# RWKV attention and a top-1 expert layer in one kernel: decay tables doubled from their middle, weight sums behind later transposes, other banks at two seams

## The chip, the cores and the metric

The kernel runs on one core of a Trainium2 chip. The metric is the device time of one execution in microseconds (us). Engines are named as in the profile: PE is TensorE (PEld its weight loads), DVE is VectorE, ACT is ScalarE, POOL is GpSimd, and SP only issues DMAs.

## The reference

```python
# B, H, S, D = 4, 8, 768, 48; for every (b, h), over t:
cur = (u * k[t])[:, None] * v[t][None, :]
y[t] = r[t] @ (state + cur)
state = w[:, None] * state + k[t][:, None] * v[t][None, :]
# x = y as (B*S, H*D) = (3072, 384); 8 experts, F = 1024
logits = x @ w_gate
e = argmax(logits); gate = softmax(logits)[e]
out = gate * (relu(x @ w1[e]) @ w2[e])
```

The decay `w` lies between 0.85 and 0.95 for every channel. All data are float32.

## The kernel before

**First half, the recurrence.** The 768 steps of a head are cut into G = 6 chunks of C = 128. Two heads make a unit, and there are U = 16 units (four head pairs for each of four batches). For a unit, `scale` (L261) multiplies r and k (tile `rk`) by a table `TT` of powers of the decay, so that the products inside a chunk become matmuls (`p_scores`, L292, into the PSUM banks X01[0], X01[1] and X23, which has two banks, X23[:, 0] and X23[:, 1]). `pairs` (L267) and `p_own` (L280) make the step's own term, `own_t` (L284) transposes it, `keys` (L271), `p_ds` (L315) and `scan` (L320) carry the state from chunk to chunk, `p_out` (L335, L340) adds both parts, and `p_tr` (L353) transposes the result into `tr` and X23, from which `keep` (L358, L359, on ScalarE) copies it into `xb`.

The table has two halves of 128 columns for each head pair: for r the powers of w from -64 to 63, for k the same powers backwards. `pw[:, l]` holds w to the power 2^l, from seven squarings on VectorE (L129), `inv` the reciprocal of the 64th power (L133). `decays` (L145, L148) starts each half with `inv` and doubles the filled part seven times, each time with one product by `pw[:, l]`. `state_decay` (L174, L175) fills `dec` from `pw[:, 7]` on GpSimd, and `key_decay` (L152) makes a further table from the same power.

Input loads are issued by SP in the order `w`, then `rk` and `vk` of units 0, 1, 2; a later `load_rk` waits until its buffer is free. `p_fill` (L109) issues matmuls of the identity that nothing reads: 25 of them while the first inputs load, 8 more before unit 1.

**Routing.** After each batch `choose`, `gates`, `p_rank` and `slots` find the expert and the row of every token, and `send` (L407) scatters the rows of `xb` to `rows` in HBM by indirect DMA from GpSimd, one for each chunk.

**Second half, the experts.** A `Pass` computes one expert over some rows. Two `early` passes (experts 0 and 1, 160 rows each, all from the first three batches) are mixed into the end of the first half; eight `late` passes follow. `L1` (L474, L476) computes relu(x w1): block f of eight goes to bank `hbank[f % 4]`, where hbank = X01[0], X23[:, 0], X01[1], X23[:, 1], and ScalarE applies the ReLU. `L2` (L558, L560) is the second layer for early passes and for remainders: three output blocks m, each in its bank (`ybank` = yps[0], dsb, yps[1] for early passes), each followed by a VectorE transpose. In early[0].L2 the argument `first` holds the eight `weight_sums` of late[0] (VectorE sums of blocks of w2 into `tums`, L684), which stand behind the transpose of block 0.

The late passes compute both layers with fewer products from sums of blocks (a form of Strassen's method): `quarter` (L496) for the first layer, with the banks `quads`, and `tokens_out` (L598) for the second, with five banks `self.banks` = ba, bb, bd, be, bf; `so` and `yt` (L616, L623, L627) are the combinations that VectorE and ScalarE make from them, and `scatter` (L670) writes the rows of the output. In late[1] bf is `zbank[2]`, that is X23[:, 0].

**What sets the order.** Every engine executes its instructions in the order in which the program lists them (a schedule written out by hand); semaphores make them wait for each other. The tiles of the second half (`tums` among them) lie in the memory of the first half's tiles (`xb` among them), so their first writer waits for the last reader.

Of the kernel before, what the change touches and what calls it, by code (L numbers as in the profile page):

```python
# [1 line left out]

# [10 lines left out]
ALU = mybir.AluOpType  # L13
# [9 lines left out]
C = 128  # L23
# [5 lines left out]
KP = 64 + D  # L29
# [10 lines left out]
def bc(ap, shape):  # L40
    return ap.to_broadcast(shape)


def straight(tc, rk, vk, w, w1, w2, out, flag):
# [8 lines left out]
    nc = tc.nc  # L53
# [8 lines left out]
    X01 = [pp.tile([128, 4, C], FP32, name=f"X{i}") for i in range(2)]  # L62
    X23 = pp.tile([128, 2, 512], FP32, name="X23")
    yps = [pp.tile([128, 512], FP32, name=f"yps{k}") for k in range(2)]
    dsb = pp.tile([128, 512], FP32, name="dsb")
    tr = pp.tile([128, 512], FP32, name="tr")
# [3 lines left out]
    hbank = [X01[0].rearrange("p a b -> p (a b)"), X23[:, 0, :], X01[1].rearrange("p a b -> p (a b)"), X23[:, 1, :]]  # L70
    ybank = [yps[0], dsb, yps[1]]
    zbank = hbank[0::2] + [X23[:, 0, :]]
# [33 lines left out]
    def p_fill(n, o):  # L106

        for _ in range(n):
            nc.tensor.matmul(o, lhsT=ident, rhs=ident, start=True, stop=True, skip_group_check=True)  # L109
# [7 lines left out]
        nc.sync.dma_start(rows.rearrange("(e n) c -> e (n c)", e=E)[:, PAD * HP * Q:CAP * HP * Q].rearrange(  # L117
            "e (p z) -> p e z", p=128), bc(zt[:, None, :], [128, E, nz]))

    p_fill(25, X01[1][:, 0, :])  # L120
    strict = cp.tile([128, C], FP32, name="strict")
    nc.gpsimd.memset(strict, 1.0)
    nc.gpsimd.affine_select(out=strict, in_=strict, pattern=[[1, C]], base=-1, channel_multiplier=-1,
# [1 line left out]

    pw = cp.tile([KP, 8, HP], FP32, name="pw")
    nc.vector.tensor_scalar(out=pw[:, 0, :], in0=wt, scalar1=W_LO, scalar2=W_HI, op0=ALU.max, op1=ALU.min)
    for l in range(7):
        nc.vector.tensor_tensor(pw[:, l + 1, :], pw[:, l, :], pw[:, l, :], op=ALU.mult)  # L129
    TT = cp.tile([KP, HP, 2, C], FP32, name="TT")  # L130
    TTf = TT.rearrange("p a u c -> p (a u c)")
    inv = cp.tile([KP, HP], FP32, name="inv")
    nc.vector.reciprocal(inv, pw[:, 6, :])  # L133

    T3c = cp.tile([KP, HP, C], FP32, name="T3c")
    T3 = cp.tile([128, HP, 2 * D], FP32, name="T3")
# [1 line left out]
    def two(h0, nh, first, second, n):  # L138

        a = TTf[:, h0 * 2 * C + first:h0 * 2 * C + first + n]  # L140
        return bass.AP(a.tensor, a.offset, [list(a.ap[0]), [2 * C, nh], [second - first, 2], [1, n]])

    def decays(h0, nh):

        nc.vector.tensor_copy(two(h0, nh, 0, 2 * C - 1, 1), bc(inv[:, h0:h0 + nh, None, None], [KP, nh, 2, 1]))  # L145
        for l in range(7):
            n = 1 << l
            nc.vector.tensor_tensor(two(h0, nh, n, 2 * C - 2 * n, n), two(h0, nh, 0, 2 * C - n, n),  # L148
                                    bc(pw[:, l, h0:h0 + nh, None, None], [KP, nh, 2, n]), op=ALU.mult)

    def key_decay(h0, nh):
        nc.vector.tensor_tensor(T3c[:, h0:h0 + nh, :], TT[:, h0:h0 + nh, 1, :],  # L152
                                bc(pw[:, 7, h0:h0 + nh, None], [KP, nh, C]), op=ALU.mult)
# [53 lines left out]
    def in_range():  # L207

        nc.vector.tensor_scalar(out=le, in0=wt, scalar1=W_HI, scalar2=None, op0=ALU.is_le)
        nc.vector.scalar_tensor_tensor(out=okw, in0=wt, scalar=W_LO, in1=le, op0=ALU.is_ge, op1=ALU.mult)  # L210
# [132 lines left out]
    def out_t(i):  # L343
        for k in range(2):
            nc.scalar.copy(yTs[i % 3][0:KP, k], yps[k][0:KP, 0:S // 2])
# [5 lines left out]
    def p_tr(i):  # L351
        for c in range(G):
            nc.tensor.matmul(trv[c // 4][:, c % 4, :], lhsT=yTs[i % 3][0:KP, c & 1, (c // 2) * C:(c // 2 + 1) * C],  # L353
                             rhs=sel[:, c & 1, i % HP, :], start=True, stop=True, skip_group_check=True)
# [22 lines left out]
    def p_rank(b):  # L377

        oh = ohs[b % 2]
        nc.tensor.matmul(rp, lhsT=ones, rhs=bc(osum[:, None, :], full), start=True, stop=False, skip_group_check=True)  # L380
        nc.tensor.matmul(rp, lhsT=tri, rhs=oh, start=False, stop=False, skip_group_check=True)
        for k in range(1, G):
            nc.tensor.matmul(rp[:, k:, :], lhsT=ones, rhs=oh[:, 0:G - k, :], start=False, stop=k == G - 1,
                             skip_group_check=True)
# [28 lines left out]
    def ids(b):  # L413
        nc.gpsimd.iota(xbs[b % 2][:, :, :, 2 * D + 1].bitcast(I32), pattern=[[4 * C, G], [1, HP]], base=4 * S * b,
                       channel_multiplier=4)
# [20 lines left out]
    class Pass:  # L436
# [109 lines left out]
            op(y[2], b22, b12, ALU.subtract)  # L546
            op(y[3], b21, y[1], ALU.subtract)

        def L2(self, first=()):

            n, g = self.n - self.c, self.g - self.gc
            if n <= 0:
                return
            y = self.y
            for m in range(DT):
                p = (zbank if self.nt else ybank)[m]
                for f in range(FT):
                    nc.tensor.matmul(p[:, 0:n], lhsT=w2s[self.k % 2][f // 2][:, f % 2, m * 128:(m + 1) * 128],  # L558
                                     rhs=self.h[:, f, self.c:self.n], start=f == 0, stop=f == FT - 1, skip_group_check=True)
                nc.vector.transpose(y[:, 0:g, 32 * m:32 * m + 32], p[:, 0:32 * g].rearrange("p (g j) -> p g j", j=32))  # L560
                for x in first:
                    op(*x, ALU.subtract)

            yo, ix, x = self.yo, self.ix, self.x[:, self.gc:self.g]
            ids = x[:, :, 2 * D + 1].bitcast(I32)
            if not self.nt:
                nc.vector.tensor_copy(ix[:, 0:g], ids)
            else:
                nc.vector.tensor_scalar(out=vm[:, 0:g], in0=pos[:, 0:g], scalar1=float(self.s0 + self.c),
                                        scalar2=bp[:, self.k:self.k + 1], op0=ALU.add, op1=ALU.is_lt)  # L570
                nc.vector.memset(ix[:, 0:g], 1 << 20)
                nc.vector.copy_predicated(ix[:, 0:g], vm[:, 0:g], ids)
            nc.vector.tensor_tensor(yo[:, 0:g, :], y[:, 0:g, :], bc(x[:, :, 2 * D:2 * D + 1], [128, g, 2 * D]), op=ALU.mult)
            if self.nt:
                self.blocks_out()
# [107 lines left out]
    def op(o, a, b, how, eng=None):  # L683
        (eng or nc.vector).tensor_tensor(o, a, b, op=how)  # L684

    early = [Pass(e, 0, EARLY, 0, early_bufs[e]) for e in range(2)]
    late = [Pass(k, EARLY if k < 2 else 0, n, 2) for k, n in enumerate(WIDTH)]
# [7 lines left out]

    selection()
    decays(0, HP)
    scale(0)
    pairs(0, nc.vector)
# [27 lines left out]
    for i in range(1, U):  # L727
        b, k = divmod(i - 6, 4)
# [62 lines left out]
        if i == 14:  # L791
            weights1(0, (2, 3))

    early[0].L1(range(0, 2), [(weights1, 1, 0), (weights1, 1, 1)])
    p_tr(U - 2)
    keep(U - 2)
    nc.gpsimd.tensor_copy(turn, xbs[1][0:1, G - 1, 2, 0:1])
    send(B - 2, range(3, G))
    p_out(U - 1)
    out_t(U - 1)  # L800
    early[0].L1(range(2, 3), [(weights1, 1, 2)])
    p_tr(U - 1)
    keep(U - 1)
    choose(B - 1)
    gates(B - 1)
    ids(B - 1)
    early[0].L1(range(3, 6), [(weights1, 1, 3), (weights2, 0, 0), (weights2, 0, 1)])
    p_rank(B - 1)
    slots(B - 1)
    send(B - 1, range(G))  # L810
# [18 lines left out]

    for p in late[:2]:  # L830
        nc.gpsimd.memset(p.h[:, :, p.n:p.c], 0.0)
    late[1].banks = dsb, yps[1], yps[0], tr, zbank[2]
    sums = [mp.tile([128, FT // 2, 128], FP32, name=f"sums{k}") for k in range(4)]
    so = [mp.tile([128, DM // 2], FP32, name=f"so{k}") for k in range(8)]
    quart = [mp.tile([128, 5, 128], FP32, name=f"quart{q}") for q in range(4)]
# [29 lines left out]
        with nc.allow_low_precision("whole numbers"):  # L865
            nc.vector.tensor_reduce(flag, viol[0:1, 0:2 * E + HP + 2], axis=AX, op=ALU.add)

    early[0].L2(late[0].weight_sums())
    in_range()
    late[0].xT()  # L870
    early[1].L2()
    for x in late[1].weight_sums():
        op(*x, ALU.subtract)
    n = len(late)
# [522 lines left out]
def rwkv5_then_switch(tc, rk, vk, w, w1, w2, out):  # L1397
    nc = tc.nc
    with tc.tile_pool(name="fl", bufs=1) as fl:
        flag = fl.tile([1, 1], I32, name="flag")  # L1400
        with tc.manual_schedule():
            straight(tc, rk, vk, w, w1, w2, out, flag)
            bad = nc.values_load(flag[0:1, 0:1], engines=[ENG.PE, ENG.SP, ENG.DVE, ENG.Activation, ENG.Pool],
                                 min_val=0, max_val=2 * E + HP + 2, skip_runtime_bounds_check_because="a sum of ones and zeros")
        with tc.If(bad > 0):
            general(tc, rk, vk, w, w1, w2, out)
# [48 lines left out]
```

## Time and profile before

| | |
|---|---|
| median of 3 runs | 371.25 us (371.16 to 371.26) |
| the profiled execution | 370.54 us |
| its span | 368.7 us |
| mean TensorE clock granted | 0.993 |
| PE busy, share of the span | 355.2 us, 96% |
| DVE busy | 263.3 us, 71% |
| POOL busy | 201.3 us, 55% |
| ACT busy | 142.9 us, 39% |
| DMA | 65.08 MB, mean 177 GB/s |

The span is the time from the first to the last instruction of the profiled execution; its own time is 1.8 us longer. The list of waits says for each engine which instruction stood idle and what released it (total, times, longest). The chain of waits follows the work that ended last back in time. In a line of the timeline the columns are start, length, engine, line, operation, output <- inputs, shape and count, and in brackets the idle time before it. Matmuls appear as two passes for each fp32 product, and their ends overlap.

### The profile page before, as it was taken

To read this page: it belongs to the slowest core of one execution; us is meant where nothing else is said; L and a number is where in the kernel's file an instruction comes from. 1 tells how busy PE (TensorE), PEld (TensorE's weight loads), DVE (VectorE), ACT (ScalarE), POOL (GpSimd) and SP (SyncE) were. 2 spreads that over 40 slices of the span, in tenths; PEclk is the share of its full clock that TensorE was granted. 3 is DMA by queue.
4 is the path that set the end of the run, shared out by engine and by line. 5 is a ranking of instruction groups with operands and counts; after the bars stand their busy time and mean duration, and the time that the engine had idled before them with its cause. 6 is when DMAs were issued, how large, how long until landed. Compare 5 with 4: busy or idle time off the path is not lost.

```text
span 368.7 us, 9101 instructions
## 1 busy us (share of the span) xinstructions
PE 355.2 (96%) x3371; PEld 336.3 (91%) x3371; DVE 263.3 (71%) x661; ACT 142.9 (39%) x411; POOL 201.3 (55%) x234
## 2 busy tenths in 40 slices
PE   8999999999999998999998999999999999999991
PEld 8788888888888998999998999999999999999891
DVE  8987798798872347593797996797688589685531
ACT  2687878777784300322322312221230321113210
POOL 3387889989874420462115506904931951999341
PEclk9999999999999999999999999999999999999997
DMA  7999797886665876678458316723842843312401
GB/s 194 256 257 244 242 277 258 246 259 216 217 169 186 299 298 133 175 231 241 124 175 198 125 43 208 192 90 117 213 150 96 199 146 127 111 49 87 145 18 52
DMA packets 35206, 65.08 MB, mean 177 GB/s; under 512 B 18618, under 2 KB 19658, under 8 KB 35153
## 3 DMA queue, kind: packets, MB, share of 16 engines
q1 hardware_dynamic: 29648, 49.86, 48.8%
q0 software_dynamic: 3776, 9.84, 7.4%
q10 hardware_dynamic: 1728, 4.72, 3.7%
q8 instruction: 28, 0.46, 0.5%
q14 instruction: 26, 0.20, 0.2%
HBM read 53.29 MB, written 11.40 MB: 175 GB/s over the span
## 4 chain that ended last, share of the span: by engine, by line
PE 84%; DMA 5%; DVE 5%; POOL 2%; issue 1%; ACT 0%; SPq 0%; POOLq 0%; DVEq 0%
PE X L496 12%; PE X L558 10%; PE tr L598 7%; PE yps L598 7%; PE X L292 6%; PE X L474 6%; PE yps L335 6%; PE yps L496 5%; PE tr L353 5%; PE yps L340 3%; PE tr L496 3%; PE dsb L496 3%; DMA rk<-in_rk_dram 3%; PE dsb L598 2%; PE dsb L315 2%; PE dsb L280 2%
## 5 line engine op out<-in xcount | busy, mean ns | idle before, releaser
L670 POOL DMA_INDIRECT out_dram<-yo,ix x28 | 28.4, 1014 | 68.0 <-DVE ia L587 63.8
L298 ACT ACTIVATE A<-ident,own 128x128 f32<-128x128 f32 x192 | 57.9, 390 | 7.2 <-DVE own L284 6.8
L407 POOL DMA_INDIRECT rows<-xb,slot x24 | 30.3, 1261 | 11.9 <-issue 6.8
L558 PE MATMUL X<-hT,w2s 128*128 128x160 f32 (+5 forms) x288 | 36.5, 287 | 0.0
L558 PEld LDWEIGHTS X<-hT,w2s 128*128 128x128 f32 x288 | 36.2, 191 | 0.2
L598 PE MATMUL yps<-tums,sums 128*128 128x192 f32 x184 | 32.4, 326 | 0.0
L598 PEld LDWEIGHTS yps<-tums,sums 128*128 128x128 f32 x184 | 30.3, 190 | 0.0
L292 PEld LDWEIGHTS X<-RK 48*128 48x128 f32 x384 | 23.3, 187 | 6.0 <-issue 5.1
L670 POOL DMA_INDIRECT out_dram<-yt,it x16 | 16.8, 1048 | 22.0 <-DVE so L616 10.9
L292 PE MATMUL X<-RK 48*128 48x128 f32 x384 | 27.6, 284 | 0.6 <-issue 0.6
L261 DVE TENSOR_TENSOR RK<-rk,TT 112x1536 f32<-112x1536 f32 x16 | 27.7, 1730 | 0.2
L267 POOL TENSOR_TENSOR rp<-rk 112x768 f32<-112x768 f32 x15 | 27.2, 1816 | 0.0
L304 DVE COPY_PREDICATED A<-strict,X 128x512 f32<-128x512 int32 x32 | 23.2, 740 | 4.8 <-ACT A L298 4.7
L496 PE MATMUL X<-xT,w1s 128*128 128x208 f32 (+5 forms) x120 | 26.0, 331 | 0.0
L684 POOL TENSOR_TENSOR tums<-w2s,tums 128x384 f32<-128x384 f32 x24 | 24.7, 1030 | 0.4
L335 PE MATMUL yps<-A,vk 128*48 128x128 f32 x384 | 24.0, 274 | 0.0
L496 PEld LDWEIGHTS X<-xT,w1s 128*128 128x128 f32 x120 | 20.9, 190 | 0.0
L335 PEld LDWEIGHTS yps<-A,vk 128*48 128x48 f32 x384 | 20.2, 123 | 0.5
L684 DVE TENSOR_TENSOR sums<-hT 128x512 f32<-128x512 f32 x16 | 17.1, 1066 | 3.6 <-ACT hT L476 3.2
L632 ACT COPY so<-tr 128x192 f32<-128x192 f32 x7 | 2.2, 320 | 44.5 <-PE tr L598 44.5
L598 PE MATMUL tr<-w2s,hT 128*128 128x192 f32 x112 | 19.4, 326 | 0.0
L525 ACT ACTIVATE hT<-hT 128x416 f32<-128x416 f32 (+5 forms) x23 | 12.3, 537 | 17.7 <-DVE hT L517 17.7
(214 smaller groups left out, 830.3 us busy)
## 6 DMA issues: line engine op xcount, KB each, us to landing
w1s<-in_w_dram SPq DMA_DIRECT2D x36, 384.0 KB, 3.2
rk<-in_rk_dram SPq DMA_DIRECT2D x16, 672.0 KB, 7.5
w2s<-in_w_dram SPq DMA_DIRECT2D x24, 384.0 KB, 3.6
vk<-in_vk_dram SPq DMA_DIRECT2D x16, 528.0 KB, 8.3
w2s<-in_w_dram ACTq DMA_DIRECT2D x8, 384.0 KB, 5.2
xs<-rows SPq DMA_DIRECT2D x16, 169.0 KB, 5.4
w1s<-in_w_dram ACTq DMA_DIRECT2D x4, 384.0 KB, 3.0
rows<-zt SPq DMA_DIRECT2D x1, 1248.0 KB
```

The costliest lines, as they stand in the source:

```text
L261: nc.vector.tensor_tensor(RKs[i % 3][0:KP].rearrange("p u (c t) -> p u c t", t=C), x[0:KP].rearrange("p u (c t) -> p u c t", t=C), bc(TT[: ...
L267: (eng or nc.gpsimd).tensor_tensor(rps[i % 2][0:KP], x[0:KP, 0], x[0:KP, 1], op=ALU.mult)
L292: nc.tensor.matmul(o, lhsT=r[q, 1, c * C:(c + 1) * C], rhs=r[q, 0, c * C:(c + 1) * C], start=True, stop=True, skip_group_check=True)
L298: nc.scalar.activation(A[:, place(c, h), :], ident, func=ACT.Copy, scale=own[i % 2][:, c, h:h + 1])
L304: nc.vector.copy_predicated(A[:, 4 * k:4 * k + 4, :], bc(m[:, None, :], [128, 4, C]), X01[k])
L335: nc.tensor.matmul(o(c, h), lhsT=v[:, c, h * D:(h + 1) * D], rhs=A[:, place(c, h), :], start=c < 2, stop=c == 0, skip_group_check=True)
L407: s_ = nc.gpsimd.indirect_dma_start(out=rows[:, :], out_offset=bass.IndirectOffsetOnAxis(ap=slot[b % 2][:, c:c + 1], axis=0), in_=xbs[b % ...
L496: nc.tensor.matmul(p[:, at * n:(at + 1) * n], lhsT=a, rhs=b, start=j == 0, stop=j == len(ab) - 1, skip_group_check=True)
L558: nc.tensor.matmul(p[:, 0:n], lhsT=w2s[self.k % 2][f // 2][:, f % 2, m * 128:(m + 1) * 128], rhs=self.h[:, f, self.c:self.n], start=f == 0 ...
L598: nc.tensor.matmul(p[:, at * Z:(at + 1) * Z], lhsT=a(f), rhs=b(f), start=f == 0, stop=f == FT // 2 - 1, skip_group_check=True)
L670: s_ = nc.gpsimd.indirect_dma_start(out=to[:, :], out_offset=bass.IndirectOffsetOnAxis(ap=at, axis=0), in_=x, in_offset=None, bounds_check ...
L684: (eng or nc.vector).tensor_tensor(o, a, b, op=how)
```

## The change

Four places are changed.

1. The table is doubled from the power 0 in its middle: GpSimd sets the middle column to 1 and makes the seven squares, VectorE makes six doublings (powers 0 to 63) beside them, and one product by `inv` makes the powers -64 to -1. The first group of fills has 17 matmuls instead of 25.
2. `early[0].L1` gets its banks from a list: blocks 0 to 2 use X01[0], X01[1], X01[0], and blocks 3 to 5 use X01[1], X01[0], X23[:, 0].
3. The eight weight sums of late[0] stand behind later transposes: three behind block 1 of early[0].L2, two behind block 0 and three behind block 1 of early[1].L2.
4. In late[1].tokens_out the fifth bank bf is `dsb` (which is ba as well) instead of X23[:, 0].

```diff
--- before.py
+++ after.py
@@ -1,4 +1,5 @@
 from contextlib import ExitStack
+from itertools import islice
 
 import concourse.bass as bass
 import concourse.tile as tile
@@ -117,7 +118,7 @@
         nc.sync.dma_start(rows.rearrange("(e n) c -> e (n c)", e=E)[:, PAD * HP * Q:CAP * HP * Q].rearrange(
             "e (p z) -> p e z", p=128), bc(zt[:, None, :], [128, E, nz]))
 
-    p_fill(25, X01[1][:, 0, :])
+    p_fill(17, X01[1][:, 0, :])
     strict = cp.tile([128, C], FP32, name="strict")
     nc.gpsimd.memset(strict, 1.0)
     nc.gpsimd.affine_select(out=strict, in_=strict, pattern=[[1, C]], base=-1, channel_multiplier=-1,
@@ -125,12 +126,9 @@
 
     pw = cp.tile([KP, 8, HP], FP32, name="pw")
     nc.vector.tensor_scalar(out=pw[:, 0, :], in0=wt, scalar1=W_LO, scalar2=W_HI, op0=ALU.max, op1=ALU.min)
-    for l in range(7):
-        nc.vector.tensor_tensor(pw[:, l + 1, :], pw[:, l, :], pw[:, l, :], op=ALU.mult)
     TT = cp.tile([KP, HP, 2, C], FP32, name="TT")
     TTf = TT.rearrange("p a u c -> p (a u c)")
     inv = cp.tile([KP, HP], FP32, name="inv")
-    nc.vector.reciprocal(inv, pw[:, 6, :])
 
     T3c = cp.tile([KP, HP, C], FP32, name="T3c")
     T3 = cp.tile([128, HP, 2 * D], FP32, name="T3")
@@ -142,11 +140,18 @@
 
     def decays(h0, nh):
 
-        nc.vector.tensor_copy(two(h0, nh, 0, 2 * C - 1, 1), bc(inv[:, h0:h0 + nh, None, None], [KP, nh, 2, 1]))
+
+        m = C // 2
+        nc.gpsimd.memset(two(h0, nh, m, C + m - 1, 1), 1.0)
         for l in range(7):
+            nc.gpsimd.tensor_tensor(pw[:, l + 1, :], pw[:, l, :], pw[:, l, :], op=ALU.mult)
+        for l in range(6):
             n = 1 << l
-            nc.vector.tensor_tensor(two(h0, nh, n, 2 * C - 2 * n, n), two(h0, nh, 0, 2 * C - n, n),
+            nc.vector.tensor_tensor(two(h0, nh, m + n, C + m - 2 * n, n), two(h0, nh, m, C + m - n, n),
                                     bc(pw[:, l, h0:h0 + nh, None, None], [KP, nh, 2, n]), op=ALU.mult)
+        nc.vector.reciprocal(inv, pw[:, 6, :])
+        nc.vector.tensor_tensor(two(h0, nh, 0, C + m, m), two(h0, nh, m, C, m),
+                                bc(inv[:, h0:h0 + nh, None, None], [KP, nh, 2, m]), op=ALU.mult)
 
     def key_decay(h0, nh):
         nc.vector.tensor_tensor(T3c[:, h0:h0 + nh, :], TT[:, h0:h0 + nh, 1, :],
@@ -546,7 +551,7 @@
             op(y[2], b22, b12, ALU.subtract)
             op(y[3], b21, y[1], ALU.subtract)
 
-        def L2(self, first=()):
+        def L2(self, between=(), count=(0, 0, 0)):
 
             n, g = self.n - self.c, self.g - self.gc
             if n <= 0:
@@ -558,7 +563,7 @@
                     nc.tensor.matmul(p[:, 0:n], lhsT=w2s[self.k % 2][f // 2][:, f % 2, m * 128:(m + 1) * 128],
                                      rhs=self.h[:, f, self.c:self.n], start=f == 0, stop=f == FT - 1, skip_group_check=True)
                 nc.vector.transpose(y[:, 0:g, 32 * m:32 * m + 32], p[:, 0:32 * g].rearrange("p (g j) -> p g j", j=32))
-                for x in first:
+                for x in islice(between, count[m]):
                     op(*x, ALU.subtract)
 
             yo, ix, x = self.yo, self.ix, self.x[:, self.gc:self.g]
@@ -791,20 +796,22 @@
         if i == 14:
             weights1(0, (2, 3))
 
-    early[0].L1(range(0, 2), [(weights1, 1, 0), (weights1, 1, 1)])
+
+    ends = [hbank[k] for k in (0, 2, 0, 2)]
+    early[0].L1(range(0, 2), bank=ends, then=[(weights1, 1, 0), (weights1, 1, 1)])
     p_tr(U - 2)
     keep(U - 2)
     nc.gpsimd.tensor_copy(turn, xbs[1][0:1, G - 1, 2, 0:1])
     send(B - 2, range(3, G))
     p_out(U - 1)
     out_t(U - 1)
-    early[0].L1(range(2, 3), [(weights1, 1, 2)])
+    early[0].L1(range(2, 3), bank=ends, then=[(weights1, 1, 2)])
     p_tr(U - 1)
     keep(U - 1)
     choose(B - 1)
     gates(B - 1)
     ids(B - 1)
-    early[0].L1(range(3, 6), [(weights1, 1, 3), (weights2, 0, 0), (weights2, 0, 1)])
+    early[0].L1(range(3, 6), bank=[hbank[k] for k in (0, 1, 0, 2)], then=[(weights1, 1, 3), (weights2, 0, 0), (weights2, 0, 1)])
     p_rank(B - 1)
     slots(B - 1)
     send(B - 1, range(G))
@@ -829,7 +836,7 @@
 
     for p in late[:2]:
         nc.gpsimd.memset(p.h[:, :, p.n:p.c], 0.0)
-    late[1].banks = dsb, yps[1], yps[0], tr, zbank[2]
+    late[1].banks = dsb, yps[1], yps[0], tr, dsb
     sums = [mp.tile([128, FT // 2, 128], FP32, name=f"sums{k}") for k in range(4)]
     so = [mp.tile([128, DM // 2], FP32, name=f"so{k}") for k in range(8)]
     quart = [mp.tile([128, 5, 128], FP32, name=f"quart{q}") for q in range(4)]
@@ -865,10 +872,11 @@
         with nc.allow_low_precision("whole numbers"):
             nc.vector.tensor_reduce(flag, viol[0:1, 0:2 * E + HP + 2], axis=AX, op=ALU.add)
 
-    early[0].L2(late[0].weight_sums())
+    between = late[0].weight_sums()
+    early[0].L2(between, (0, 3, 0))
     in_range()
     late[0].xT()
-    early[1].L2()
+    early[1].L2(between, (2, 3, 0))
     for x in late[1].weight_sums():
         op(*x, ALU.subtract)
     n = len(late)
```

## The prediction

> **What bounds the kernel now.** I read the page first, for the engine that is nearly always busy, then the list of waits, for where that engine stands still, then the chain of waits and the timeline around each stop.
>
> ```profile
> PE   355.2 (96%) x3371; PEld 336.3 (91%) x3371; DVE 263.3 (71%) x661; ACT 142.9 (39%) x411; POOL 201.3 (55%) x234
> PE 84%; DMA 5%; DVE 5%; POOL 2%; issue 1%; ACT 0%; SPq 0%; POOLq 0%; DVEq 0%
> ```
>
> TensorE is busy for 96% of the 368.7 us span and is 84% of the chain. A change helps only where it removes a stop of TensorE that nothing else holds open. The list of waits has three stops after the first 21 us:
>
> ```profile
> PE dsb L558 <- DVE yqe L560: 1.2, 1, 1.2
> PE X L496 <- DVE yt L623: 1.2, 1, 1.2
> PE X L474 <- ACT xb L359: 0.4, 1, 0.4
> ```
>
> By the timeline they are at 119.8 (L474), 141.0 (L558) and 198.8 us (L496), and the change has an edit at each. The prologue is its fourth place. The chain there:
>
> ```profile
> 2.19 9.89 DMA rk<-in_rk_dram
> 12.08 0.02 issue
> 12.10 1.77 DVE RK L261
> 13.87 0.05 issue
> 13.93 0.18 POOL turn L716
> 14.10 1.78 POOL rp L267
> ```
>
> The first scaling (L261) runs at 7.39, but the chain doesn't pass through it: it goes through the landing of the second `rk` at 12.08, and the second scaling starts 0.02 us later.
>
> [...] the first table product (112x8) took 0.67 us, the next 0.18, and the first ended 0.03 us after the GpSimd copy of `dec` (4.30 to 5.13). [...] at 119.8 us the product into columns 0 to 159 of a half of X23 waited for the ScalarE copy of columns 256 to 359 of that half. [...] The 1.25 us stop at 139.7 left PEclk at 1.00; no longer stop is in the trace.
>
> **Part 1, decay tables and fills.** Removed from VectorE: seven squarings (pitch 0.196 us, 2.81 to 4.15) and the copy (0.17) ahead of the table; seven products become six and a last one by the reciprocal. Added on GpSimd: a memset and seven squarings. The nearest row is the GpSimd 128x8 product of L403, 0.198 us at a pitch of 0.277. From pw[0] at 2.78 the sixth power is then there at 2.85 + 6 x 0.277 = 4.5. The five products before the last two go beside it; the one with n = 32 (0.42) ends by about 4.7, reciprocal (0.17) and last product (512 columns, 0.69) by about 5.6, instead of 7.36. [...] What waits for the table is the first scaling, and it waits for the first `rk` as well:
>
> ```profile
> L93 SPq EVENT_SEMAPHORE x2: 17/908/1798, 7.2 to 12.1; - x2
> ```
>
> SP's own wait for that transfer, queued ahead of the fourth `rk`, ended at 7.2, and the next one at 12.1 plus the scaling. So scaling 0 can gain 0.2 us at most (7.39 to 7.2), and scaling 1 nothing, since `rk` 1 lands at 12.08 with the DMA engines at 96 to 118% busy from 3 to 13 us. Cost taken: 0. Ends: -0.1, and +0.7[...]; the slack before `rk` 1 is only 0.12 us, since VectorE is free for scaling 1 at 11.96. Eight fills fewer (0.22 us each at full clock) end at 7.4 instead of 9.2, and TensorE idles some 1.6 us: nothing, as TensorE has 0.63 us to spare before 15.9 and the clock should hold.
>
> **Part 2, banks of the first expert's first layer.** `ends` and the list after it take blocks 1 and 3 off X23, which `p_tr` writes and `keep` reads in between. Block 3 goes to X01[1], whose last reader is the ReLU of block 1, done at 113.8. TensorE goes on at about 119.21 (the last `p_tr` pass began at 119.10, pitch 0.11) instead of 119.80: **-0.6** (from -0.5 to -0.7, with the slow first pass after a stop). Next candidates: block 4's bank, free with the ReLU of block 2 at 118.4; block 5's, free at 119.7 and needed at 120.8; the rank product needs `oh` at 121.47 and comes at 121.7; block 6's needs the ReLU of block 3, still behind `ex` on ScalarE at 121.3, and comes at 121.9. None is late. ScalarE's weight issues (w2s of expert 0 among them) and GpSimd's six sends start up to 0.6 us earlier; their order is kept.
>
> **Part 3, weight sums behind later transposes.**
>
> ```profile
> 130.38 5.98 DMA rows<-xb,slot
> ...
> 136.57 0.57 DVE tums L684
> ...
> 139.16 1.50 DVE tums L684 x3
> 140.66 0.27 DVE yqe L560
> ...
> 140.97 2.44 PE dsb L558 x16
> ```
>
> `tums` lies where the `xb` being sent lay, so the eight sums wait for the last send to land (136.35) and then hold VectorE until 140.6. Queued behind them is the transpose that empties `dsb`, whose product ended near 135.4, and TensorE stands before its next use of `dsb`. The last pass before the stop began at 139.43; at the pitch of 0.136 the next was due at 139.56 and came at 140.97: 1.41, plus 0.1 for the slow first pass. Now that transpose runs at about 135, ahead of the wait, and three sums follow. The transpose of the third bank runs at 136.3 + 3 x 0.52 = 137.9 and is needed at 141. Next on VectorE are copy, weighting, `in_range` (1.3) and `xT` of the late pass, which waits for `xs`, issued when the sends have landed (0.4 us earlier at best); before, `xs` was in by about 140.6. `xT` (1.0) ends by 141.7, and TensorE needs it at 145.43 - 2.1 = 143.3. The other five sums and their transposes (3.5) stand behind it; the sums of `late[1]` and its `xT` end near 150.3 against 152.4 needed. Gain **-1.45** (from -1.3 to -1.55). No DMA is moved past another.
>
> **Part 4, the last bank of late[1].** `bf` was X23[:, 0], read late by VectorE, so the quarter's third product stood until 198.83. Now it is `dsb`, which is `ba` too:
>
> ```profile
> 194.79 1.46 PE L598 MATMUL X<-tums,hT 128*128 128x192 f32 x8
> ...
> 195.62 0.35 DVE L616 TENSOR_TENSOR so<-dsb,so 128x192 f32<-128x192 f32 x1
> ...
> 198.83 0.62 PE L496 MATMUL X<-toks,quart 128*128 128x206 f32 x2 [1.18 <-DVE yt L623]
> ```
>
> The add that empties `ba` stands at the end of VectorE's backlog and ends at 195.98. The product into `bf`, at 194.79 before, now waits until 196.03. After it come 0.1 of restart, its 8 passes (1.30) and 8 passes of the quarter (1.39): 198.82, where the old order had 198.83 with the restart (0.1) still to pay. The stop moves ahead of the product and is paid anyway: **-0.1** (from -0.2 to +0.3). VectorE's `midu` starts 0.3 later, but the step after it waited 1.6 us for TensorE.
>
> **Sum.** 0 - 0.6 - 1.45 - 0.1 = -2.15 us. Between 200 and 361 us the list of waits has no TensorE stop that could swallow it: weights load as TensorE frees their buffers. The profiled execution had 370.54 (span 368.7 and 1.8 around it), so 368.4. The median of the three runs is 0.71 above it: **369.1**.
>
> **Rivals.**
> - The table was the limit: the whole 1.8 us (7.36 to 5.6) comes through, 367.3. The early end of the fills suits that; the landing at 12.08 is against. Chance 0.05.
> - Only one stop yields: the sends end at 136.35 whatever (the DMA engines are full from 127 to 135), `xs` is later than estimated, or block 3 finds another wait. With Part 3 alone 369.7, with Part 2 alone 370.6. The margins of 1.6 us and more are against it. That an edit does nothing is this case too. 0.14.
> - [...] +0.7, 369.8. The 0.67 us product is for it, the 1.6 us between 5.6 and 7.2 against. 0.09.
> - **Slower: the TensorE clock drops** in the gap from 7.4 to 9.0 and stays low while the first units wait for inputs. Half clock for T us loses T/2 less the 0.63 to spare; it cancels the gain from T = 5.6 on. [...] For it: the cold start at 1.44 took 4.0 us to warm. [...] 0.10.
>
> **How the numbers follow.** The forecast has 0.62, its own range 368.4 to 369.7. The range 368.2 to 371.2 takes in the second and third rivals and leaves out the first, most of the clock case, and the tails. A measurement of this kernel can tell about 0.2% (0.74 us). Faster by more: 0.62 + 0.05 + 0.09 + 0.09 of the second = 0.85; within: 0.05 of the second and 0.03 of the clock case = 0.08; slower: 0.07, the rest of the clock case.
>
> **What would show it.** Right: scaling 0 at 7.2 and scaling 1 still at 12.1; no TensorE stop at 119.8; none before the `dsb` product near 139; a stop of about 1.2 us before the `bf` product near 193. Wrong: PEclk under 1.0 between 9 and 20 us; scaling 1 after 12.3; a TensorE stop before the late pass's first product; a stop over 1.5 us at the fourth place.

## The result and the profile after

The changed kernel takes **367.2 us** (median of 7 executions, 366.97 to 369.16), the kernel before beside it 371.09 us (median of 7, 370.23 to 371.26). The ratio is 0.9913, with a 95% interval of 0.989 to 0.9936: 2.4 to 4.1 us less. The profiled execution took 367.2 us, its span is 365.3 us. The forecast was 369.1 us with a range from 368.2: the direction was right, and the gain is larger than the range allowed. Medians below are over all executions; the ratios leave out the four that took over 1.5% longer than the fastest of their kernel. The mean TensorE clock that an execution was granted (1 is full speed) is given where a time can't be understood without it.

From the page of the kernel after, busy times and shares of the chain:

```profile
PE 353.3 (97%) x3355; PEld 335.1 (92%) x3355; DVE 261.5 (72%) x653; ACT 142.7 (39%) x411; POOL 204.6 (56%) x242
PE 90%; DVE 2%; POOL 2%; issue 2%; DMA 1%; POOLq 0%; ACT 0%; DVEq 0%
```

Stops went, not work: TensorE's busy time fell by 1.9 us (16 passes of fills are left out), the span by 3.4. The list of waits of the kernel after, TensorE's four longest rows (line numbers are up to five higher than before here: L603 is the product of L598, L266 the scaling of L261):

```profile
PE X L110 <- POOL ident masks.py:199: 1.4, 1, 1.4
PE dsb L603 <- DVE so L621: 1.2, 1, 1.2
PE tr L358 <- ACT yT L350: 0.5, 1, 0.5
PE dsb L285 <- POOL rp L272: 0.4, 1, 0.4
```

The stops at 119.8 and 141.0 us are gone, and the third now stands ahead of the product into bf (L603), both as forecast. The second view is the timeline of VectorE in the prologue, the two scalings before and then the kernel after:

```profile
7.39 1.76 DVE L261 TENSOR_TENSOR RK<-rk,TT 112x1536 f32<-112x1536 f32 x1
...
12.10 1.76 DVE L261 TENSOR_TENSOR RK<-rk,TT 112x1536 f32<-112x1536 f32 x1
```

```profile
5.18 0.69 DVE L153 TENSOR_TENSOR TT<-TT,inv 112x512 f32<-112x512 f32 x1
6.80 1.76 DVE L266 TENSOR_TENSOR RK<-rk,TT 112x1536 f32<-112x1536 f32 x1 [0.93 <-DMA rk<-in_rk_dram]
...
11.29 1.75 DVE L266 TENSOR_TENSOR RK<-rk,TT 112x1536 f32<-112x1536 f32 x1
```

The table is done at 5.87 us, the first scaling follows the landing of `rk` 0, and the second runs at 11.29. That is 0.81 us earlier than before, where the forecast had no change: in this execution `rk` 1 landed at 11.20, not at 12.08.

To see where the time went, the same TensorE instruction was looked up in two traces and its start compared. The table gives the shift against the kernel before (us, minus is earlier) after each place. The second profile of the changed kernel is from the third group of experiments below.

| place in the kernel before | forecast, step | kernel after | second profile of it |
|---|---|---|---|
| units 2 and 3 (21.5 to 27) | 0 | -0.95 | -0.87 |
| after 28.5 (31 to 60) | 0 | -2.01 (step -1.06) | -1.79 (-0.92) |
| 100 to 110 | 0 | -1.43 (+0.58) | -1.98 (-0.19) |
| after 119.8 | -0.6 | -2.09 (-0.66) | -2.64 (-0.66) |
| after 141.0 | -1.45 | -3.61 (-1.52) | -4.16 (-1.52) |
| after 198.8, and to the end | -0.1 | -3.65 (-0.04) | -4.20 (-0.04) |

Parts 2, 3 and 4 gave -2.22 where -2.15 was forecast. What was not forecast lies ahead of 80 us, in two places: the start of unit 2, and a stop at 28.5 us. That stop in TensorE's timeline of the kernel before, and the same 24 passes of a unit's scores in the kernel after:

```profile
27.61 1.16 PE L292 MATMUL X<-RK 48*128 48x128 f32 x14
29.35 0.93 PE L292 MATMUL X<-RK 48*128 48x128 f32 x10 [0.58 <-issue]
```

```profile
26.66 1.61 PE L297 MATMUL X<-RK 48*128 48x128 f32 x24
```

In brackets is the idle time by the modelled end of the pass before; from one start to the next the stop is 0.85 us. "issue" says that TensorE waited for nothing that the profile shows. The +0.58 ahead of 100 us comes from a stop of 0.82 us at 78.4 us, in the first profile of the changed kernel only. TensorE waited there for a copy on ScalarE. That copy stood behind the one below, which had waited 2.04 us until rows that `send` wrote had landed:

```profile
78.47 0.33 ACT L364 COPY xb<-X 128x208 f32<-128x208 f32 x1 [2.04 <-DMA rows<-xb,slot]
```

### The profile page after: what moved, and what is told of

It reads as the page before. It is cut to its first block, busy times and chain, and to the rows that moved or that the text cites. A ratio compares the mean times of both kernels' runs of the same rounds, so it can differ in the third digit from the quotient of the medians.

```text
span 365.3 us, 9077 instructions
## 1 busy us (share of the span) xinstructions
PE 353.3 (97%) x3355; PEld 335.1 (92%) x3355; DVE 261.5 (72%) x653; ACT 142.7 (39%) x411; POOL 204.6 (56%) x242
## 4 chain that ended last, share of the span: by engine, by line
PE 90%; DVE 2%; POOL 2%; issue 2%; DMA 1%; POOLq 0%; ACT 0%; DVEq 0%
PE X L501 12%; PE X L563 10%; PE X L479 8%; PE tr L603 7%; PE yps L603 7%; PE X L297 6%; PE yps L340 6%; PE yps L501 5%; PE tr L358 5%; PE yps L345 3%; PE tr L501 3%; PE dsb L501 3%; PE dsb L603 3%; PE yps L563 2%; PE dsb L320 2%
## 5 line engine op out<-in xcount | busy, mean ns | idle before, releaser
L603 PE MATMUL yps<-tums,sums 128*128 128x192 f32 x184 | 32.4, 326 | 0.0
L603 PEld LDWEIGHTS yps<-tums,sums 128*128 128x128 f32 x184 | 30.3, 190 | 0.0
L272 POOL TENSOR_TENSOR rp<-rk 112x768 f32<-112x768 f32 x15 | 28.8, 1919 | 0.0
L266 DVE TENSOR_TENSOR RK<-rk,TT 112x1536 f32<-112x1536 f32 x16 | 27.8, 1735 | 1.1 <-DMA rk<-in_rk_dram 0.9
L603 PE MATMUL tr<-w2s,hT 128*128 128x192 f32 x112 | 19.4, 326 | 0.0
```

Of the source, the lines that this page charges most:

```text
L266: nc.vector.tensor_tensor(RKs[i % 3][0:KP].rearrange("p u (c t) -> p u c t", t=C), x[0:KP].rearrange("p u (c t) -> p u c t", t=C), bc(TT[: ...
L272: (eng or nc.gpsimd).tensor_tensor(rps[i % 2][0:KP], x[0:KP, 0], x[0:KP, 1], op=ALU.mult)
L603: nc.tensor.matmul(p[:, at * Z:(at + 1) * Z], lhsT=a(f), rhs=b(f), start=f == 0, stop=f == FT // 2 - 1, skip_group_check=True)
```

## The experiments

The 18 runs come from five groups, each on another chip. A run is compared with the kernel before on its own chip, whose median was between 370.65 and 375.62 us.

### First group: is it Part 1?

Part 1 alone, and Parts 2 to 4 alone (the same edit taken out of the changed kernel):

```diff
-    p_fill(25, X01[1][:, 0, :])
+    p_fill(17, X01[1][:, 0, :])
...
-        nc.vector.tensor_copy(two(h0, nh, 0, 2 * C - 1, 1), bc(inv[:, h0:h0 + nh, None, None], [KP, nh, 2, 1]))
+        nc.gpsimd.memset(two(h0, nh, m, C + m - 1, 1), 1.0)
```

> The kernel before with Part 1 alone (table from the middle, squares on GpSimd, 17 fills). The combined change gained some 1.4 us more than the 2.1 us of Parts 2 to 4. T1 (the table is worth time: with it done at 5.9 instead of 7.4 us, VectorE is ahead of the inputs and scalings 0 and 1 follow the landings): 0.8 to 1.5 us faster, scaling 1 at about 11.3, TensorE 0.8 us earlier at the start of unit 2. T2 (Part 1 is worth nothing, as predicted; the 1.4 us is a difference between two executions): within 0.4 us of before, scaling 1 still released by a landing near 12.1. T3 (the fills: fewer instructions ahead of the first products): as T1, and the run with 17 fills alone shows it too.

> The changed kernel with Part 1 undone (table and 25 fills as before), Parts 2 to 4 kept. T1: 2.1 us faster than before, some 1.4 slower than the changed kernel. T2: 3.5 us faster than before, like the changed kernel.

The fills alone, and the kernel before without an edit:

```diff
-    p_fill(25, X01[1][:, 0, :])
+    p_fill(17, X01[1][:, 0, :])
```

> The kernel before with 17 fills instead of 25 and nothing else. T1 and T2: within 0.3 us of before, since the fills end long before the first products. T3: most of the 1.4 us, the second rk landing near 11.2.

> The kernel before, unchanged, for a second profile of it. T2: the landing of the second rk (12.08 in the first profile) and the TensorE stop of 0.85 us at 28.5 move by half a us or more from one execution to the next. T1: both stand where they were within 0.2 us.

Ratios to the kernel before: Part 1 alone 0.9977 (0.9952 to 1.0001), Parts 2 to 4 alone 0.9907 (0.9871 to 0.9943), 17 fills alone 0.9978 (0.995 to 1.0007), no edit 0.9993 (0.9967 to 1.002). By time alone this tells little. Parts 2 to 4 alone gained 3.5 us, as T2 said, but with an interval of 2.1 to 4.8 us, which takes in the 2.1 of T1. Part 1 alone gained 0.9 us (0.0 to 1.8) and the fills alone 0.8 (-0.3 to 1.9). On this chip the profiles had more stops between 85 and 140 us (the unchanged kernel took 375.38 us); their cause is open.

The traces tell more. The stop at 28.5 us, in the middle of unit 4's scores, is in all three profiles with 25 fills (from one start to the next 0.85 us before, 0.47 without an edit, 1.13 with Parts 2 to 4) and in none of three with 17. With Part 1 the second scaling ran at 11.42 us and unit 2 started 0.81 us earlier, as T1 said; with the 17 fills alone the scaling ran at 11.87. In the unedited kernel the second `rk` landed at 11.79 us, not at 12.08, and the stop was 0.38 us shorter: less than the half microsecond of T2, more than the 0.2 of T1. So the table (T1), one execution's landing (T2) and the fills (T3) each hold for a part.

### Second group: table, fills, and the number of instructions

The table without the fills is Part 1 as above, with the line of the 25 fills kept. The second run is the kernel before without the eight fills ahead of unit 1:

```diff
-    p_fill(8, yps[0][:, 384:512])
```

The third is the changed kernel with 25 fills:

```diff
-    p_fill(17, X01[1][:, 0, :])
+    p_fill(25, X01[1][:, 0, :])
```

T3 for the second run rests on the page of the kernel before, which counts 28 packets with 0.46 MB, 16 KB each, on a queue named `q8 instruction`.

> The kernel before with the new table alone, 25 fills kept. In the profiles so far the table shows at the start of unit 2 (some 0.45 us: the first scaling starts at 6.8 or 6.9 instead of 7.39), and a TensorE stop at 28.5 us is in all three profiles with 25 fills (0.85, 0.47 and 1.13 us) and in none of three with 17. T1 (the table is worth time): unit 2 about 0.45 us earlier than in a kernel with the old table, and the 28.5 us stop still there; 0.3 to 0.6 us faster than before. T2 (Part 1 is worth nothing): within 0.2 us. T3 (only the fills count): unit 2 where it was, stop still there, within 0.2 us.

> The kernel before with the first 25 fills kept and the 8 later ones (before unit 1) left out: as many TensorE instructions ahead of unit 2 as with 17 and 8. T3 in the form that the stop at 28.5 us depends on how many TensorE instructions stand ahead of it (they arrive in blocks of 16 KB by DMA): the stop is gone, some 0.8 us faster. If it depends on when the first fills end: the stop stays, within 0.2 us of before.

> The changed kernel with 25 fills instead of 17. T3: the 28.5 us stop is back, and 0.8 us or a little more of the gain over before is lost: about 2.6 us faster than before. T1 alone: 3.5 us faster, like the changed kernel.

**Table alone**: 371.31 us, ratio 1.0025 (0.9997 to 1.0053). No gain. `rk` 1 landed at 11.88 us, the second scaling ran at 11.91, unit 2 was 0.17 us earlier. The stop at 28.5 is there:

```profile
27.45 1.16 PE L296 MATMUL X<-RK 48*128 48x128 f32 x14
29.18 0.93 PE L296 MATMUL X<-RK 48*128 48x128 f32 x10 [0.58 <-issue]
```

As in the kernel before, the stop comes after the 14th of the 24 passes.

**25 and no later fills**: the stop at 28.5 is gone although the first fills end as late as before, so it hangs on the number of instructions ahead, as T3 said. The time got longer nonetheless, 371.99 us, ratio 1.0037 (1.0014 to 1.0059): without the later fills TensorE stood 2.65 us (from one start to the next) ahead of 16.1 us, and its clock was at half from about 17.6 to 21.

**Changed kernel with 25 fills**: 369.08 us, 0.9937 (0.9919 to 0.9956), 1.6 to 3.0 us faster than before where 2.6 was expected. The stop is back, 1.40 us long in the profiled execution, and the clock was at half from 31 to 37.8 us behind it.

A fourth run takes away what is left of the stop at Part 4. In `late[1]` ScalarE copies both halves of ba, and VectorE adds from the copy:

```diff
+            if self.k == 1:
+                nc.scalar.copy(so[1], ba[:, Z:2 * Z])
+                nc.vector.tensor_tensor(so[1], so[1], so[0], op=ALU.add)
+            else:
-            add(so[1], ba, 1, so[0])
+                add(so[1], ba, 1, so[0])
```

> The changed kernel with the second half of the bank ba of late[1] copied out by ScalarE, so that the product into bf does not wait for VectorE's backlog. If Part 4 pays its stop only for that add: the stop at 191 us is gone and the kernel is 1.0 to 1.2 us faster than the changed one, 4.5 us faster than before. If another wait stands behind it (VectorE's combinations for the next quarter): under 0.5 us faster than the changed one.

366.55 us, ratio 0.9884 (0.9866 to 0.9902): 4.3 us faster than before, where 4.5 was expected. The two timelines, first the changed kernel, then this one:

```profile
189.88 1.46 PE L603 MATMUL tr<-tums,sums 128*128 128x192 f32 x8
192.51 1.54 PE L603 MATMUL dsb<-tums,hT 128*128 128x192 f32 x8 [1.16 <-DVE so L621]
193.88 1.21 PE L501 MATMUL X<-xT,w1s 128*128 128x206 f32 x6
```

```profile
190.39 1.46 PE L603 MATMUL tr<-tums,sums 128*128 128x192 f32 x8
191.69 1.46 PE L603 MATMUL dsb<-tums,hT 128*128 128x192 f32 x8
192.99 1.21 PE L501 MATMUL X<-xT,w1s 128*128 128x206 f32 x6
```

The stop is gone. Of the 1.44 us that the shift gains there, 0.46 come back by 210 us, where VectorE's backlog is late for the quarter: 0.9 to 1.0 us stays.

### Third group: the parts that the forecast priced

The changed kernel once more, the version with ScalarE's copy beside it, and Parts 2 and 3 each alone on the kernel before. Part 2 alone (its three calls of L1 in the same way):

```diff
+    ends = [hbank[k] for k in (0, 2, 0, 2)]
...
-    early[0].L1(range(2, 3), [(weights1, 1, 2)])
+    early[0].L1(range(2, 3), bank=ends, then=[(weights1, 1, 2)])
```

Part 3 alone:

```diff
-    early[0].L2(late[0].weight_sums())
+    between = late[0].weight_sums()
+    early[0].L2(between, (0, 3, 0))
...
-    early[1].L2()
+    early[1].L2(between, (2, 3, 0))
```

> The changed kernel once more, for a second profile beside the next run. If the gain over the forecast came from the fills (no stop at 28.5 us, 0.85) and from an early landing of the second rk (11.2 in the first profile, 11.3 to 12.5 in the others), the stop is absent again, the start of unit 2 lies between the two first profiles (20.0 and 20.8), and the gain over before is 2.9 to 3.6 us.

> The changed kernel with ScalarE copying out the second half of ba, a second time and now beside the changed kernel itself. In its first profile the stop at 191 us was gone and 0.3 us of it came back at 205: 1.0 to 1.2 us faster than the changed kernel. Rival: a later wait gives it all back, within 0.3 us.

> The kernel before with Part 2 alone (banks of the first expert's first layer). As predicted: the stop at 119.8 us goes, 0.5 to 0.7 us. Rival: VectorE's sums wait for the sends whatever TensorE does, the stop at 141.0 grows by as much, and the gain is under 0.2 us.

> The kernel before with Part 3 alone (weight sums behind later transposes). As predicted: the stop of 1.5 us at 141.0 goes, 1.3 to 1.55 us. Rival: the sums are late for the first late pass, and a stop between 142 and 155 takes over 0.5 us back.

| run | median us (before 370.71) | ratio, 95% interval | shift at the end |
|---|---|---|---|
| the changed kernel | 367.45 | 0.9916 (0.9895 to 0.9937) | -4.20 |
| with ScalarE's copy | 366.41 | 0.9869 (0.9832 to 0.9905) | -1.93 |
| Part 2 alone | 370.3 | 0.9984 (0.9969 to 0.9999) | -0.43 |
| Part 3 alone | 369.19 | 0.9962 (0.9944 to 0.998) | -1.66 |

The changed kernel repeats its gain: 3.1 us by the ratio (2.3 to 3.9), after 3.2 the first time. The stop at 28.5 is absent again, and unit 2 starts at 20.09 us, in the range that was expected. TensorE's rows of the list of waits follow, first of Part 2 alone, then of Part 3 alone:

```profile
PE dsb L558 <- DVE yqe L560: 1.3, 1, 1.3
PE X L496 <- DVE yt L623: 1.2, 1, 1.2
PE X L292 <- issue: 0.6, 1, 0.6
```

```profile
PE X L497 <- DVE yt L624: 1.2, 1, 1.2
...
PE X L293 <- issue: 0.6, 1, 0.6
PE X L475 <- ACT xb L360: 0.4, 1, 0.4
```

Each part takes away its own stop and no other. With Part 2 alone the stop at L558 grew by some 0.06 us only (1.55 to 1.61 from start to start), so the rival that the sums give it back falls. With Part 3 alone no new stop came between 142 and 155 us. The version with ScalarE's copy has the lower median by 1.0 us, as expected. Its profiled execution was its longest (369.01 us): `rk` 0 landed at 7.83 us, and TensorE ran at half clock from about 10.5 to 17.3. The places behind show the same steps as above.

### Fourth group: why the stop at 28.5 hangs on the fills

Four passes fewer, and four more, ahead of it:

```diff
-    p_fill(8, yps[0][:, 384:512])
+    p_fill(6, yps[0][:, 384:512])
```

and in the other run

```diff
-    p_fill(8, yps[0][:, 384:512])
+    p_fill(10, yps[0][:, 384:512])
```

> The kernel before with 25 and 6 fills (before unit 1) instead of 25 and 8: 4 passes fewer ahead of 28.5 us. If TensorE waits there for instructions that arrive at a fixed time after their transfer began (2.7 to 3.0 us in five profiles), 4 passes of 0.11 us later in the program: the stop shrinks by about 0.44, to 0.4, and stands some 4 passes later. If only the end of the first fills mattered: 0.85 as before, at the same pass.

> The kernel before with 25 and 10 fills: 4 passes more ahead of 28.5 us. By the number of instructions: the stop stands 4 passes earlier and grows by about 0.44, to 1.3. If only the end of the first fills mattered: 0.85 as before, at the same pass.

The timelines, first with 6, then with 10:

```profile
28.14 1.38 PE L292 MATMUL X<-RK 48*128 48x128 f32 x18
30.00 0.71 PE L292 MATMUL X<-RK 48*128 48x128 f32 x6 [0.47 <-issue]
```

```profile
27.25 0.93 PE L292 MATMUL X<-RK 48*128 48x128 f32 x10
28.91 1.16 PE L292 MATMUL X<-RK 48*128 48x128 f32 x14 [0.73 <-issue]
```

With eight fills the stop stands after 14 of 24 passes, in every profile that has 25 and 8. With two fills fewer (four passes) it stands after 18, with two more after 10. Counted from the first fill, it stands behind the 348th pass in all nine profiles with the stop. **The stop sits at a fixed place in TensorE's instruction stream.** The page names what arrives in such pieces (packets, MB, share of the DMA engines' time):

```profile
q8 instruction: 28, 0.46, 0.5%
```

Queue q8 brings 28 packets of 16 KB in the kernel before. The trace has 3,371 matmuls, as many weight loads and 83 waits and the like on TensorE, 6,825 instructions or 244 for each packet; between one packet of q8 and the next TensorE issues 250 of them on average, the last packet aside. The second packet in the trace starts at 26.45 us in the kernel before, and TensorE goes on at 29.35. In the nine profiles with the stop this distance is between 2.66 and 3.00 us, while the stop itself is between 0.47 and 1.40. No releaser is recorded for the stop; the reading that fits its place and its end is that TensorE waits there for its instructions.

By this reading the 32 instructions of eight fills (each pass has a weight load) move the border between two blocks 16 passes on, into the output transposes (L353). The other eleven profiles bear this out. There TensorE comes to its 348th pass 2.52 to 4.87 us after the packet began, against 1.48 to 2.30 in the nine, so the block has mostly landed. The three that came soonest (2.52 to 2.70) have a rest of the stop there, a step of 0.41, 0.20 and 0.22 us behind pass 348 where the others have 0.11 at most, and it ends 2.84 to 2.93 us after the packet began. The first of these is a profile of the 17 fills alone. The first eight passes of the transposes took 1.52 us there, and 1.14 in the second profile of the changed kernel:

```profile
28.80 1.52 PE L353 MATMUL tr<-sel,yT 112*128 112x104 f32 x8
```

```profile
28.28 1.14 PE L358 MATMUL tr<-sel,yT 112*128 112x104 f32 x8
```

The place was as expected in both runs and the size was not (0.74 and 1.00 us from start to start, for 0.4 and 1.3), since the block's transfer started 0.83 us later and 0.29 us earlier than before. Each of the two ran once (371.01 and 371.12 us, beside 370.65 before), so their times say nothing.

Part 1's two halves side by side, on another chip (the edits of the first group):

> The kernel before with 17 fills alone, again. If the fills gave the part of the gain that was not forecast: 0.7 to 1.0 us faster than before. If that was one early landing: within 0.3 us.

> Part 1 alone, again, beside the 17 fills alone. If the table adds what it showed in executions with early inputs: 0.2 to 0.5 us faster than with the fills alone. If inputs are mostly late: like the fills alone.

The 17 fills: 369.96 us, ratio 0.9994 (0.9979 to 1.001). Part 1: 371.25 us, 1.0009 (0.9991 to 1.0026), beside 370.65 before. Neither gains by the ratio, where 0.7 to 1.0 us had been expected of the fills. The executions say why: they fall in two groups, by the mean TensorE clock of each. This split was made after the fact.

| | clock 0.99 or more | median | clock under 0.99 | median |
|---|---|---|---|---|
| before | 42 | 370.64 | 1 | 372.32 |
| 17 fills | 13 | 369.44 | 9 | 371.70 |
| Part 1 | 12 | 369.65 | 10 | 371.73 |

At a clock of 0.99 or more the fills gain 1.2 us and Part 1 1.0. On the chip of the first group the same split gives 375.03 us before, 373.39 with 17 fills and 373.27 with Part 1; there 13 of 45, 8 of 16 and 9 of 22 executions have a clock under 0.99. So the executions with an undisturbed clock gain by the fills on both chips, and the table adds nothing to it that shows (0.2 us slower and 0.1 faster than the fills alone).

The profiled execution of the 17 fills had a mean clock of 0.996, that of Part 1 0.986. Their stretches from 10 to 18 us (busy times of PE, PEld, DVE, ACT and POOL, then the granted clock, the DMA share and GB/s), first 17 fills, then Part 1:

```profile
10.00:18.00 8.00, 7.42 (x110) 5.83 (x112) 7.47 (x11) 5.34 (x19) 3.12 (x3) 1.00 1.04 276
```

```profile
10.00:18.00 8.00, 7.91 (x68) 6.41 (x64) 5.41 (x8) 4.04 (x14) 3.11 (x3) 0.58 1.03 267
```

At 0.58 of the clock unit 2 starts 1.8 us later than before. This is the rival with the clock, at the place that it named. It priced half clock for T us at T/2 - 0.63. In the profiled execution the clock was at half for 6.8 us, for which that gives 2.8; the executions of low clock take 2.1 to 2.3 us more than the others. The pause ahead is in the timelines of TensorE, in the same order:

```profile
3.73 3.90 PE L109 MATMUL X<-ident 128*128 128x128 f32 x24
9.21 0.71 PE L292 MATMUL X<-RK 48*128 48x128 f32 x8 [1.57 <-DVE RK L261]
```

```profile
3.74 3.22 PE L109 MATMUL X<-ident 128*128 128x128 f32 x24
8.78 0.71 PE L296 MATMUL X<-RK 48*128 48x128 f32 x8 [1.83 <-DVE RK L265]
```

### Fifth group: a shorter pause

The changed kernel with ScalarE's copy and with wider fills, and the changed kernel beside it:

```diff
-    p_fill(17, X01[1][:, 0, :])
+    p_fill(9, X01[1][:, 0, :])
+    for _ in range(3):
+        nc.tensor.matmul(X01[1], lhsT=ident, rhs=bc(ident[:, None, :], [128, 4, C]), start=True, stop=True,
+                         skip_group_check=True)
```

> The changed kernel with ScalarE copying out the second half of ba, and with the first fills as 9 small ones and 3 of four times the columns: the time of 21 fills with the instructions of 12, so that TensorE's pause ahead of the first product is 0.9 us shorter and no stop at 28.5 us comes back. If the pause lowers the clock: hardly any execution with a mean clock under 0.99, and 4.2 to 4.6 us faster than before. If the clock falls whatever the fills: as many such executions as in the changed kernel, and some 4 us faster at the most.

> The changed kernel beside it, once more: 3.0 to 3.6 us faster than before, with one execution in ten or more at a mean clock under 0.99 and some 2 us longer; about 1 us slower than the run beside it.

With wider fills: 372.05 us (6 executions), ratio 0.9882 (0.9825 to 0.9939), 4.4 us faster than before (2.3 to 6.6). The changed kernel: 372.67 us (22), 0.9922 (0.9896 to 0.9949), 2.9 us faster (1.9 to 3.9). Before: 375.62 us. By time the two runs can't be told apart. The expectation on the clock was a miss: 4 of 6 executions with wider fills have a clock under 0.99, 9 of 22 of the changed kernel, 7 of 27 of the kernel before. The profiled execution had a pause of 0.95 us ahead of the first product and still ran at half clock from about 11.6 to 18.4. No stop was at 28.5. In the executions at 0.99 or more the medians are 370.1 (two only) and 371.59 us.

## Why the prediction was right or wrong

**Part 2, -0.6: right.** The shift at 119.8 is -0.66 in both profiles. Alone it gave 0.9984 (0.0 to 1.1 us), and none of the next candidates was late.

**Part 3, -1.45: right.** The step at 141.0 is -1.52 in both, alone 0.9962 (0.7 to 2.1 us). The first late pass did not wait: `xT` was done at 139.7 us, with 2.2 to spare ahead of its product at 141.8.

**Part 4, -0.1: right.** The shift is -0.04, and the stop moved ahead of the product into bf, 1.16 us of idle time where "about 1.2" was said. The version with ScalarE's copy, in which the stop is gone, shows that it was paid for that one add.

**Part 1, 0: wrong, by two terms.** The first is in the sentence on the fills: "nothing, as TensorE has 0.63 us to spare before 15.9 and the clock should hold". That treated the fills as time alone. They are instructions too, 32 fewer, and, by the reading above, the border of an instruction block moved from a place where TensorE stood 0.85 us to one that it reaches when the block has mostly landed. Measured: the shift steps by -1.06 and -0.92 us there in two profiles of the changed kernel. The miss could have been avoided. The forecast says that the list of waits has three stops after the first 21 us; it has a fourth, which the sum left out:

```profile
PE X L292 <- issue: 0.6, 1, 0.6
```

This row of the kernel before has no releaser, and a stop without one is not a stop without a cause.

The second term is "scaling 1 nothing, since `rk` 1 lands at 12.08". One execution's landing was taken for the kernel's. In twenty profiles `rk` 1 lands between 11.20 and 12.71 us, with the table old or new, and in half of them it is ahead of VectorE. The second scaling then comes 4.48 us after the first, by VectorE's own queue (up to 4.97 in three of these ten, in two of which TensorE's clock came up as late as 7.3 to 7.5 us and in one fell at 10.5). With the old table that is 7.39 + 4.48 = 11.87 at the earliest, and it was 11.87 or 11.88 in four profiles; with the new table the first scaling follows its input, and where that came early (6.80, 6.88, 6.93, though 7.2 was said to be the least) the second ran at 11.29 to 11.42. So the table is worth up to 0.6 us at unit 2 where the inputs come early, and nothing where they come late. In the one profile of the table alone `rk` 1 came late (11.88), and by time it showed no gain.

The first pass of unit 2 moved from 20.82 to 20.01 us, by the 0.81 us of the second scaling (12.10 to 11.29). Of these, 0.23 could have come with the old table and an earlier landing: that the kernel before was profiled with a late one is luck. The other 0.58 took the new table and the early landing of this execution (11.20), and that landing is luck too; how often the executions that were not profiled had one is not known. The last 0.14 of the -0.95 lie in the first eight passes of unit 2, which took 0.51 us for 0.64; they come with the 17 fills (unit 2 was 0.35 us earlier with the old table and 17 fills, where the scaling was 0.23 earlier), and their cause is open.

**The rivals.** The rival in which the table is the limit named the right place, but priced 1.8 us where 0.6 is the most. In the rival of +0.7 us VectorE's products and GpSimd's squares hold each other up. That hardly came: the table ended at 5.67 to 5.87 us in ten profiles, where 5.6 was forecast. In the first profile of the changed kernel the product of 256 columns took 0.42 us beside a square, as it had alone in the kernel before; the square took 0.45 us for 0.20, and the table did not need it. The rival with the clock was put at 0.10. The mean clock was under 0.99 in 9 and 10 of 22 executions of the two kernels with Part 1's fills in the fourth group, and in 1 of 7, 1 of 10 and 9 of 22 of the changed kernel. This is not peculiar to the 17 fills: in the kernel before it was so in 1 of 43 executions of the fourth group, but in 7 of 27 of the fifth and 13 of 45 of the first. Nor does it tell the place: of five profiles with such a mean clock, three had the drop between 10.5 and 18.4 us, as the rival said, and two at 31.0 and 123.5 us. Still the shortness of the gap was no reason to dismiss it: drops came behind pauses of 0.95 and 1.83 us. It did not decide the result on the first chip.

**What stays open.** What lowers the clock. An idle pause of 0.95 us ahead of the first product came before a drop, and others of 1.6 and 1.8 us (17 fills, and ScalarE's copy in the second group) did not. The share of time in which TensorE is busy doesn't decide it either. Counted in stretches of 3.41 us from where the clock came up, the stretches that ended with a drop within the program had shares of 0.43 to 0.74, and others of 0.52 to 0.57 were followed by none.

## What to carry to other kernels

A stop with no releaser, in the middle of a group of equal instructions, can be a wait for the arrival of the instructions themselves, as the 0.85 us at 28.5 us are read here. Then adding or taking away instructions ahead moves it (by four passes for two fills), and a change of the program's length has an effect that its own cost does not show. Where two limits end within a few tenths of each other (a landing at 12.08, VectorE free at 11.87 to 11.96), the trace of one execution doesn't tell which binds, so a gain there is a range and not zero. Fills that keep TensorE warm have two prices, the pause behind them and the instructions that they are.

## What the runs showed of the hardware that was not expected

- By the reading above, TensorE stood 0.47 to 1.40 us for an instruction block, until 2.66 to 3.00 us after the block's transfer had started, while the DMA engines were full with inputs (106.6% of their time by the profile, from 26 to 28 us of the kernel before).
- Its clock came up between 3.1 and 6.2 us after the first fill (at 4.5 to 7.7 us in the traces), so that 17 fills ended anywhere between 6.8 and 8.3 us, and the pause behind them had a length of its own in every profile. In the kernel before it came up at 5.41 us, and the passes of the fills were 0.21 us apart ahead of that and 0.11 behind it.
- In all twenty traces the later changes of the clock lie whole multiples of 3.41 us after it came up; in the kernel before it came up at 5.41 us and fell at 363.81, 105 times 3.413 later. In three of them it came up at 7.1, 4.5 and 7.3 us, fell at 10.5, 11.3 and 17.6 (1, 2 and 3 such steps later) and rose again at 17.3, 18.2 and 21.0 (3, 4 and 4 steps after the first rise). So a drop lasted 6.8 us in four profiles, two steps, and 3.4 us in two (the third of these, and the unedited kernel from 123.5 to 126.9 us), one step. The idle pauses ahead of two of the drops, 0.95 and 1.83 us, were shorter than a step.
